# Thresholded attention and tanh-shrink layers: shared tiles of two neighbouring pairs in one duo, and a joint product for both tiles' last keys

## The chip, the cores and the metric

The kernel runs on one core of a Trainium2 chip. The metric is the time of one execution on the device, in microseconds (us), and lower is better. The engines of the core are named as the profile names them: PE is TensorE (PEld its weight loads), DVE is VectorE, ACT is ScalarE, POOL is GpSimd, and SP is the engine whose queue sends nearly all DMAs.

## What is computed

The reference has two parts, one after the other. Attention over 8 batches x 8 heads x 576 positions x 64 dimensions keeps, in each row, only the scores within tau = 0.02 of the row's largest:

```
scores = scale * q @ k.T
thresh = max(scores, -1) - tau
scores = where(scores >= thresh, scores, -1e9)
attn = softmax(scores);  x = attn @ v
```

The result, laid out as 4608 tokens x 512, goes through two layers: `h = x @ w_in` (2048 wide), `g = h - tanh(h)`, `out = g @ w_out`.

## The kernel before

**Pairs and tiles.** Two heads of a batch make a *pair*, so there are 32 pairs. A head has 576 query rows: four tiles of 128 and a remainder of 64. The remainders of the pair's two heads stand together, 64 rows each, in one *shared* tile. So a pair has `TPP` = 9 tiles: in the kernel before j = 0 to 3 (first head), 4 (shared), 5 to 8 (second head). Tile number i counts on over all pairs to 288.

**Steps of a tile.** `scores` (L296) writes a row tile against all 576 keys into PSUM (psS, two buffers, which the transposes of k and q, ps_k and ps_q, use too): q and k are split into two fp16 halves, so a plain tile takes four matmuls (L320), and a shared tile eight with 64 output rows each (L310). VectorE copies the tile out as sc and takes its row maximum (L330). `shift` (L336) makes the threshold nb of it on VectorE (L347). `kink` (L355) runs a very steep Prelu on ScalarE (L367), which leaves z near zero where a score is kept and hugely negative elsewhere. z is then turned so that keys lie on partitions: for the first six pairs (`on_pe`) by PE transposes into psZ (L387), later by a DMA transpose on SP's queue (L375). `weights` (L377) takes the exponential, giving pT (L396 or L404). `attend` (L409) multiplies pT with the values vb, which carry a column of ones so that the row sum comes along (65 columns); the results go to psO, of which there is one buffer. `norm` (L441) divides on VectorE (L447 to L453) into osb, and `emit_x` (L460) turns a pair's osb by PE (psX, L465 and L471) into the layers' input xT and xR (copied by VectorE, L478 and L479).

**Duos.** 576 is four and a half blocks of 128 keys. Two plain tiles therefore lie side by side in one z of 1152 = 9 x 128 columns, called a *duo*: (0,1), (2,3), (5,6), (7,8), kind A the first and B the second. The middle block holds the last 64 keys of both tiles, so vb has two versions of that key block (index 4 and 5), one with zeros in the lower and one in the upper half. A shared tile (kind M) has no partner: its z is padded with hugely negative numbers to 640 columns (tiles zm, L93 to L98), has its own transpose of five blocks and its own exponential of 640 columns. Of a duo, each tile takes five value products of 65 columns, ten in all (L433); the shared tile takes five of 130 columns, for both heads' values at once, of which `own` picks the right head's half (L453).

**The order of the work** is written out by hand: each engine runs its instructions in the order in which the loop over steps s (L681) writes them, for all engines together. Step s holds `shift` of tile s + 7, `scores` of tile s + 8 (`AHEAD`), `kink` of tile s + 5, tanh of the last hidden block (`bend`, L497), `weights` of tile s, one piece of the layers, `shrink` (g on VectorE, L504), the stores that are due, `attend` of tile s - 2 with `norm` and `emit_x`, and then what the plan has for the step (`PREP`, L634): loads of k, q and v, their splitting on POOL, and the transposes `turn` (L242), which for pair p fall on steps 9p - 13 (k) and 9p - 11 (q); q of the odd pairs from 9 on and of pair 30 is turned by DMA instead, at step 9p - 13. (The first 36 tiles run their weights and attend four steps early.)

**The layers.** From pair 4 on, each stretch of 36 steps (four pairs) also works on the batch before: 16 pieces of `hidden` (four matmuls into psH, L488) and 16 of `project` (four into psY, L514), one a step, hidden on even steps, from the stretch's fifth step on; the first four steps have none. psH shares its two buffers with psX. Where a psY is complete, VectorE copies it out (yo, L524). What is left after the last tile, from 466 us, is layers alone.

Of the kernel before, what the change touches and what calls it, by code (L numbers as in the profile page):

```python
# [9 lines left out]
F32 = mybir.dt.float32  # L10
BF16 = mybir.dt.bfloat16
FP16 = mybir.dt.float16
AX = mybir.AxisListType
ALU = mybir.AluOpType
# [4 lines left out]
def kernel(  # L19
# [11 lines left out]
    nc = tc.nc  # L31
    P = 128

    B, H, S, D = q.shape
# [3 lines left out]
    tau = float(tau)  # L38
# [5 lines left out]
    STEEP = 1.0e30  # L44
# [2 lines left out]
    NPAIR = B * HPAIR  # L47
    DM_C = d_model // P
    DF_C = d_ff // P
    TPP = 9  # L50
    NTILE = NPAIR * TPP

# [18 lines left out]
    const = ctx.enter_context(tc.tile_pool(name="const", bufs=1))  # L71
# [11 lines left out]
    NV = 4  # L83
    vbs = []
    for i in range(NV):
        vb = const.tile([P, 2, 6, D + 1], BF16, name=f"vb{i}")
# [2 lines left out]
        nc.gpsimd.memset(vb[0:64, :, 4, D : D + 1], 1.0)  # L89
        nc.gpsimd.memset(vb[64:P, :, 5, D : D + 1], 1.0)  # L90
        vbs.append(vb)

    NM = 2  # L93
    zms = []
    for i in range(NM):
        zm = const.tile([P, 5 * P], BF16, name=f"zm{i}")
        nc.vector.memset(zm[:, S : 5 * P], -STEEP)
        zms.append(zm)  # L98

    mx3 = []
    for i in range(6):
        mx = const.tile([P, 8], F32, name=f"mx{i}")
# [26 lines left out]
    ps_o = pool("ps_o", 1, space=PSUM)  # L131
# [157 lines left out]
    REM = (slice(512, 576), slice(576, 640))  # L289
    scs, mxs, nbs, zs, zts, pts, ops = {}, {}, {}, {}, {}, {}, {}  # L290

    def kind(j):

        return "M" if j == 4 else "A" if j in (0, 2, 5, 7) else "B"

    def scores(i):  # L296
        p, j = divmod(i, TPP)
        qT, kT, kS = mats[p, "q"], mats[p, "k"], mats[p, "ks"]
        ps = ps_big.tile([P, 1024], F32, name="psS", tag="big")
        main, rem, lo = slice(0, 512), slice(512, 576), 0  # L300
        if kind(j) == "B":
            main, rem, lo = slice(512, 1024), slice(448, 512), 448
        if j == 4:
            qrem = REM
            if q_by_dma(p):
                qrem = (slice(512, 640, 2), slice(513, 640, 2))
            for n, kk in enumerate((kT, kS)):
                for dst, srcs in ((main, MAIN), (rem, REM)):
                    for hh in range(2):
                        nc.tensor.matmul(  # L310
                            out=ps[64 * hh : 64 * hh + 64, dst],
                            lhsT=qT[:, qrem[hh]], rhs=kk[:, srcs[hh]],
                            start=(n == 0), stop=(n == 1),
                        )
        else:
            hh = int(j > 4)
            lhs = qT[:, j * P : (j + 1) * P]
            for n, kk in enumerate((kT, kS)):
                for dst, src in ((main, MAIN[hh]), (rem, REM[hh])):
                    nc.tensor.matmul(  # L320
                        out=ps[:, dst], lhsT=lhs, rhs=kk[:, src],
                        start=(n == 0), stop=(n == 1),
                    )
        sc = sc_pool.tile([P, S], F32, name="sc")
        if kind(j) == "B":
            mx = mxs[i] = mxs.pop(i - 1)
        else:
            mx = mxs[i] = mx3[i // 2 % len(mx3)]
        c = int(kind(j) == "B")
        nc.vector.tensor_scalar(  # L330
            out=sc, in0=ps[:, lo : lo + S], scalar1=SC, scalar2=None,
            op0=ALU.mult, op1=ALU.max, accum_out=mx[:, c : c + 1],
        )
        scs[i] = sc

    def shift(i):  # L336

        kd = kind(i % TPP)
        if kd == "A":
            return  # L340
        mx = mxs.pop(i)
        nb = st_pool.tile([P, 9], F32, name="nb", tag="nb")
        o, m = nb[:, 0:1], mx[:, 0:1]
        if kd == "B":
            o = nb.rearrange("p (a b) -> p a b", b=3)[:, :, 0:2]
            m = mx.rearrange("p (a b) -> p a b", b=4)[:, :, 0:3]
        nc.vector.tensor_scalar(  # L347
            out=o, in0=m, scalar1=-1.0, scalar2=tau, op0=ALU.mult, op1=ALU.add
        )
        if kd == "B":  # L350
            nbs[i - 1], nbs[i] = nb[:, 0:1], nb[:, 1:2]
        else:
            nbs[i] = nb[:, 0:1]

    def kink(i):  # L355
        sc, nb = scs.pop(i), nbs.pop(i)
        kd = kind(i % TPP)
        if kd == "B":
            zt = zs.pop(i - 1)
            z = zt[:, S:W]  # L360
        elif kd == "A":
            zt = zs[i] = z_pool.tile([P, W], BF16, name="z")
            z = zt[:, 0:S]
        else:
            zt = zms[i // TPP % NM]
            z = zt[:, 0:S]
        nc.scalar.activation(  # L367
            out=z, in_=sc, func=ACT.Prelu, bias=nb, scale=1.0, alpha=STEEP
        )
        if on_pe(i):  # L370
            zts[i] = zt
        elif kd != "A":
            n = 5 if kd == "M" else TPP
            zts[i] = zt_pool.tile([P, TPP, P], BF16, name="zT")
            nc.sync.dma_start_transpose(out=zts[i][:, 0:n, :], in_=zt)  # L375

    def weights(i):  # L377


        kd = kind(i % TPP)  # L380
        n, off = {"A": (4, 0), "M": (5, 0), "B": (5, 4)}[kd]
        if on_pe(i):
            z = zts.pop(i)
            pl, tag = (ps_h, "h") if i % 2 and i < HPAIR * TPP else (ps_y, "y")
            ps = pl.tile([P, 5 * P], BF16, name="psZ", tag=tag)
            for c in range(n):
                nc.tensor.matmul(  # L387
                    out=ps[:, c * P : (c + 1) * P],
                    lhsT=z[:, (off + c) * P : (off + c + 1) * P],
                    rhs=ident_bf, is_transpose=True, start=True, stop=True,  # L390
                )
            if kd == "B":
                pt = pts.pop(i - 1)
            else:
                pt = p_pool.tile([P, TPP * P], FP16, name="pT")
            nc.scalar.activation(  # L396
                out=pt[:, off * P : (off + n) * P], in_=ps[:, 0 : n * P], func=ACT.Exp
            )
        elif kd == "A":
            return  # L400
        else:
            n += off
            pt = p_pool.tile([P, TPP * P], FP16, name="pT")
            nc.scalar.activation(  # L404
                out=pt[:, 0 : n * P], in_=zts.pop(i)[:, 0:n, :], func=ACT.Exp
            )
        pts[i] = pt

    def attend(i):  # L409

        p, j = divmod(i, TPP)
        kd, vb = kind(j), vbs[p % NV]
        if kd == "A":
            return
        if j in (1, 6):
            ops[p, int(j > 4)] = ps_o.tile([P, 6, D + 1], F32, name="psO", tag="o")
        po = ops[p, int(j > 4)]
        if kd == "M":
            pt = pts.pop(i)

            for c in range(5):
                nc.tensor.matmul(
                    out=po[:, 4:6, :], lhsT=pt[:, c * P : (c + 1) * P],
                    rhs=vb[:, :, c, :], start=(c == 0), stop=(c == 4),
                )
            return
        pt, hh = pts.pop(i), int(j > 4)

        for ab in range(2):
            blocks = [(4 * ab + ab + c, c) for c in range(4)]  # L430
            blocks.append((4, 4 + ab))
            for n, (blk, c) in enumerate(blocks):
                nc.tensor.matmul(  # L433
                    out=po[:, (j - 1 - 5 * hh) + ab, :],
                    lhsT=pt[:, blk * P : (blk + 1) * P], rhs=vb[:, hh, c, :],
                    start=(n == 0), stop=(n == 4),
                )

    osb = {}

    def norm(p, hh):  # L441
        po = ops.pop((p, hh))
        if hh == 0:
            osb[p] = o_pool.tile([P, 5, 2, D], BF16, name="osb")
        n = 5 - hh
        rc = st_pool.tile([P, 5], F32, name="rc", tag="rc")
        nc.vector.reciprocal(out=rc[:, 0:n], in_=po[:, 0:n, D])  # L447
        nc.vector.tensor_tensor(  # L448
            out=osb[p][:, 0:4, hh, :], in0=po[:, 0:4, 0:D],
            in1=rc[:, 0:4].unsqueeze(2).to_broadcast([P, 4, D]), op=ALU.mult,  # L450
        )
        if hh == 0:
            nc.vector.scalar_tensor_tensor(  # L453
                out=osb[p][:, 4, :, :], in0=po[:, 4:6, 0:D], scalar=rc[:, 4:5],
                in1=own, op0=ALU.mult, op1=ALU.mult,
            )
# [224 lines left out]
    for s in range(-AHEAD, NTILE + LAG + 3):  # L681
        p, j = divmod(max(s, 0), TPP)
# [36 lines left out]
        for i in atts.pop(s, []):  # L719
            pp, jj = divmod(i, TPP)  # L720
            if i < NTILE:
                attend(i)
            if i < NTILE and jj in (4, 8):
                norm(pp, int(jj > 4))
            if jj == 1 and pp:
                emit_x(pp - 1)
        for step in plan.pop(s, []):
            step()
# [61 lines left out]
```

## Time and profile before

| | |
|---|---|
| timed runs, us | 537.05, 538.59, 539.47 (median 538.59) |
| profiled execution | 537.19, of which the profile's span is 535.4 |
| granted TensorE clock | 1.0 throughout |
| sc (L330) | 288 of 752 ns, 216.2 us of VectorE |
| z (L367) | 288 of 768 to 770 ns, 218.1 us of ScalarE |
| exp after a DMA transpose (L404) | 104 of 1152 columns, 1153 ns; 26 of 640 columns, 726 ns |
| value products of duos (L433) | 1280 of 65 columns |
| value products of shared tiles (L422) | 160 of 130 columns |
| nb (L347) | 128 for duos, 155 ns; 32 for shared tiles, 144 ns |
| DMA transposes of z (L375) | 104 of duos, 26 of shared tiles |

Each row comes from the groups of instructions by line. The duration of one instruction is longer than what it takes from its engine, because the next one starts before it ends: of ten value products each lasts 193 ns, but they start about 32 ns apart. The profile's list of waits puts idle time down to the work that ended it; the chain that ended last follows the work back from the last instruction.

### The profile page before, as it was taken

The numbers are of one execution on the slowest core, as the hardware profiler recorded it, in microseconds if no ns is written. First come the engines' busy times: TensorE is split into PE (matmuls) and PEld (weight loads), VectorE is DVE, ScalarE is ACT, GpSimd is POOL, SyncE is SP. The second block draws the span as 40 slices with busy tenths as digits, with TensorE's granted clock in tenths as the row PEclk, the third lists the DMA queues.
The fourth block names the chain that finished last, engine by engine and source line by source line (L and its number), as shares of the span: only waits on it lengthen the run. The fifth ranks groups of instructions, "written<-read, shape, count | busy, mean of one in ns | idle before, by whom it ended". The sixth has DMA issues, their size and how long they took to land.

```text
span 535.4 us, 12959 instructions
## 1 busy us (share of the span) xinstructions
PE 506.0 (95%) x4704; PEld 287.7 (54%) x4771; DVE 427.1 (80%) x1201; ACT 437.9 (82%) x630; POOL 290.2 (54%) x390
## 2 busy tenths in 40 slices
PE   5999898999999999999999999999999999999997
PEld 3666565555555555555555555555555455444444
DVE  4999888989888988889888988898888888554440
ACT  4999888999898989899888989898989989543330
POOL 7999996767555666656555755566665620000000
PEclk9999999999999999999999999999999999999999
DMA  7654646999898899889998899998999985401113
GB/s 204 182 185 146 208 155 163 181 183 186 189 191 160 180 197 184 168 182 189 192 184 186 184 193 185 164 180 197 186 168 179 198 148 107 105 21 39 39 41 78
DMA packets 204768, 85.76 MB, mean 160 GB/s; under 512 B 172320, under 2 KB 197152, under 8 KB 204704
## 3 DMA queue, kind: packets, MB, share of 16 engines
q1 hardware_dynamic: 204112, 84.51, 74.8%
q8 instruction: 37, 0.61, 0.5%
q10 hardware_dynamic: 592, 0.43, 0.3%
q14 instruction: 27, 0.22, 0.1%
HBM read 36.70 MB, written 9.44 MB: 86 GB/s over the span
## 4 chain that ended last, share of the span: by engine, by line
PE 71%; DVE 16%; ACT 6%; issue 3%; DMA 3%; POOL 1%; SPq 0%; DVEq 0%; ACTq 0%; POOLq 0%
PE psY L514 20%; PE psH L488 18%; PE psS L320 16%; DVE sc L330 8%; PE psO L433 5%; PE psS L310 3%; DVE g L507 3%; ACT pT L396 3%; PE psHt L488 3%; PE ps_k L234 2%; ACT z L367 2%; DVE kT L257 2%; PE psZ L387 1%; DVE yo L524 1%; PE ps_q L234 1%
## 5 line engine op out<-in xcount | busy, mean ns | idle before, releaser
L330 DVE TENSOR_SCALAR_CACHE_REDUCE sc<-psS 128x576 f32<-128x576 f32 x288 | 216.2, 752 | 23.7 <-PE psS L320 14.2
L367 ACT ACTIVATE z<-sc,nb 128x576 bf16<-128x576 f32 x256 | 193.5, 768 | 19.7 <-DVE nb L347 19.7
L514 PE MATMUL psY<-w_out_sb,g 128*128 128x512 bf16 (+1 forms) x551 | 137.6, 373 | 3.3 <-issue 0.9
L263 POOL COPY kS<-kT 64x1152 f16<-64x1152 f16 x62 | 70.7, 1141 | 128.7 <-DVE nb L347 127.0
L404 ACT ACTIVATE pT<-zT 128x1152 f16<-128x1152 bf16 (+1 forms) x130 | 138.8, 1068 | 0.7 <-DMA zT<-z 0.7
L488 PE MATMUL psH<-xT,w_in_sb 128*128 128x512 bf16 x455 | 119.1, 379 | 3.6 <-DVE g L507 2.3
L320 PE MATMUL psS<-kT,qT 128*128 128x512 f16 (+1 forms) x512 | 104.9, 286 | 7.3 <-DVE sc L330 5.1
L501 ACT ACTIVATE th<-psH 128x512 f32<-128x512 f32 x128 | 75.3, 589 | 36.3 <-PE psH L488 33.9
L320 PEld LDWEIGHTS <-qT 128*128 128x128 f16 x1024 | 72.6, 97 | 57.0 <-issue 10.3
L320 PE MATMUL psS<-kS,qT 128*128 128x512 f16 x496 | 101.4, 286 | 0.2 <-POOL kS L263 0.2
L507 DVE SCALAR_TENSOR_TENSOR g<-th,psH 128x512 bf16<-128x512 f32 x128 | 87.3, 682 | 17.6 <-ACT th L501 17.5
L514 PEld LDWEIGHTS <-g 128*128 128x128 bf16 x592 | 50.7, 98 | 56.9 <-issue 4.0
L488 PEld LDWEIGHTS <-w_in_sb 128*128 128x128 bf16 x576 | 49.2, 98 | 58.2 <-issue 4.5
L433 PEld LDWEIGHTS <-pT 128*128 128x128 f16 x1280 | 55.7, 98 | 25.2 <-issue 1.9
L433 PE MATMUL psO<-vb,pT 128*128 128x65 bf16 x1280 | 61.2, 193 | 0.3
L187 POOL TENSOR_TENSOR qhl<-qraw,qhl 128x576 f16<-128x576 f32 x31 | 39.7, 1280 | 2.6
L187 POOL TENSOR_TENSOR khl<-kraw,khl 128x576 f16<-128x576 f32 x31 | 39.6, 1278 | 2.6
L396 ACT ACTIVATE pT<-psZ 128x640 f16<-128x640 bf16 (+1 forms) x54 | 35.5, 659 | 4.9 <-PE psZ L387 4.5
L257 DVE COPY kT<-ps_k 128x1152 f16<-128x1152 f16 x31 | 23.4, 756 | 13.6 <-PE ps_k L234 13.5
L524 DVE COPY yo<-psY 128x512 f32<-128x512 f32 (+1 forms) x31 | 21.1, 682 | 13.4 <-DMA out_dram<-yo 6.5
L448 DVE TENSOR_TENSOR osb<-psO,rc 128x256 bf16<-128x256 f32 x64 | 27.2, 424 | 2.2
L234 PE MATMUL ps_k<-ident_f,khl 128*128 128x128 f16 x288 | 22.0, 221 | 5.7 <-DVE khl L200 5.7
(78 smaller groups left out, 507.4 us busy)
## 6 DMA issues: line engine op xcount, KB each, us to landing
vraw<-in_v_dram SPq DMA_DIRECT2D x32, 256.0 KB, 3.5
out_dram<-yo SPq DMA_DIRECT2D x32, 256.0 KB, 2.7
kraw<-in_k_dram SPq DMA_DIRECT2D x31, 256.0 KB, 3.2
qraw<-in_q_dram SPq DMA_DIRECT2D x31, 256.0 KB, 3.7
wt<-in_moe_w_in_dram SPq DMA_DIRECT2D x8, 512.0 KB, 4.7
wt<-in_moe_w_out_dram SPq DMA_DIRECT2D x8, 512.0 KB, 4.2
zT<-z SPq DMA_TRANSPOSE x104, 3.5
kraw<-in_k_dram SPq DMA_DIRECT2D x32, 32.0 KB, 2.8
```

Of the source, the lines that this page charges most:

```text
L187: nc.gpsimd.tensor_tensor(out=hl[:, :, 1, :], in0=x, in1=hl[:, :, 0, :], op=ALU.subtract)
L263: nc.gpsimd.tensor_copy(out=o, in_=i)
L320: nc.tensor.matmul(out=ps[:, dst], lhsT=lhs, rhs=kk[:, src], start=(n == 0), stop=(n == 1),)
L330: nc.vector.tensor_scalar(out=sc, in0=ps[:, lo : lo + S], scalar1=SC, scalar2=None, op0=ALU.mult, op1=ALU.max, accum_out=mx[:, c : c + 1],)
L367: nc.scalar.activation(out=z, in_=sc, func=ACT.Prelu, bias=nb, scale=1.0, alpha=STEEP)
L396: nc.scalar.activation(out=pt[:, off * P : (off + n) * P], in_=ps[:, 0 : n * P], func=ACT.Exp)
L404: nc.scalar.activation(out=pt[:, 0 : n * P], in_=zts.pop(i)[:, 0:n, :], func=ACT.Exp)
L433: nc.tensor.matmul(out=po[:, (j - 1 - 5 * hh) + ab, :], lhsT=pt[:, blk * P : (blk + 1) * P], rhs=vb[:, hh, c, :], start=(n == 0), stop=(n ...
L488: nc.tensor.matmul(out=ps, lhsT=w_in_sb[:, c, n * P : (n + 1) * P], rhs=xs[m][:, c, :] if m < B else xR[:, c, :, :], start=(c == 0), stop= ...
L501: nc.scalar.activation(out=th, in_=ps, func=ACT.Tanh)
L507: nc.vector.scalar_tensor_tensor(out=gs[m][:, n, :], in0=th, scalar=-1.0, in1=ps, op0=ALU.mult, op1=ALU.add,)
L514: nc.tensor.matmul(out=ps, lhsT=gs[m][:, n, ms * P : (ms + 1) * P], rhs=w_out_sb[:, n, cols], start=(n == 0), stop=(n == DF_C - 1),)
```

## The change

The kinds now alternate over all tiles: an even i is A and an odd i is B. So that this works out, a pair of even number has its shared tile last (j = 8) and a pair of odd number has it first (j = 0, its plain tiles being j = 1 to 8). The shared tiles of pairs p and p + 1, p even, are thus neighbours, tiles 9p + 8 and 9p + 9, and make a duo like any other. The tiles zm, and what was written for kind M, are gone.

In `attend`, a duo's middle block is multiplied once with both versions of the last key block (130 columns, into both tiles' places in psO) and is the first of nine products instead of two of ten; the other eight only add. A shared duo takes five products of 130 columns for each of its two tiles, as before: those for the even pair as soon as its pT is there, those for the odd pair two steps later, when that pair's first psO is opened, so the shared pT is held for both. The five-wide `norm` (with the shared tile) is now that of the second head in even pairs and of the first head in odd pairs. `emit_x` of an even pair comes at j = 2 of the next pair; that of an odd pair stays at j = 1.

```diff
-    NM = 2
-    zms = []
-    for i in range(NM):
-        zm = const.tile([P, 5 * P], BF16, name=f"zm{i}")
-        nc.vector.memset(zm[:, S : 5 * P], -STEEP)
-        zms.append(zm)
...
-    def kind(j):
-        return "M" if j == 4 else "A" if j in (0, 2, 5, 7) else "B"
+    def kind(i):
+        return "AB"[i % 2]
+
+    def place(i):
+        p, j = divmod(i, TPP)
+        j = j - p % 2
+        return (p, None, 4) if j in (-1, 8) else (p, j // 4, j % 4)
...
-        elif kd != "A":
-            n = 5 if kd == "M" else TPP
+        elif kind(i) == "B":
             zts[i] = zt_pool.tile([P, TPP, P], BF16, name="zT")
-            nc.sync.dma_start_transpose(out=zts[i][:, 0:n, :], in_=zt)
+            nc.sync.dma_start_transpose(out=zts[i], in_=zt)
...
+        p, hh, t = place(i)
+        vb, pt = vbs[p % NV], pts[i]
+        if hh is None:
+            attend_shared(p - 1, 0, pt)
             return
-        pt, hh = pts.pop(i), int(j > 4)
-        for ab in range(2):
-            blocks = [(4 * ab + ab + c, c) for c in range(4)]
-            blocks.append((4, 4 + ab))
-            for n, (blk, c) in enumerate(blocks):
...
+        if t == 1:
+            ops[p, hh] = ps_o.tile([P, 6, D + 1], F32, name="psO", tag="o")
+            if p % 2 and hh == 0:
+                attend_shared(p, 1, pts.pop(i - 2))
+        po = ops[p, hh]
+        nc.tensor.matmul(
+            out=po[:, t - 1 : t + 1, :], lhsT=pt[:, 4 * P : 5 * P],
+            rhs=vb[:, hh, 4:6, :], start=True, stop=False, skip_group_check=True,
+        )
+        for n in range(8):
+            ab, c = divmod(n, 4)
+            blk = 5 * ab + c
+            nc.tensor.matmul(
+                out=po[:, t - 1 + ab, :], lhsT=pt[:, blk * P : (blk + 1) * P],
+                rhs=vb[:, hh, c, :], start=False, stop=(n == 7), skip_group_check=True,
+            )
+        pts.pop(i)
+
+    def attend_shared(p, ab, pt):
+        vb = vbs[p % NV]
+        for n in range(5):
+            blk, c = ((5 * ab + n, n) if n < 4 else (4, 4 + ab))
+            nc.tensor.matmul(
+                out=ops[p, 1 - p % 2][:, 4:6, :], lhsT=pt[:, blk * P : (blk + 1) * P],
+                rhs=vb[:, :, c, :], start=(n == 0), stop=(n == 4),
+            )
...
-            if i < NTILE and jj in (4, 8):
-                norm(pp, int(jj > 4))
-            if jj == 1 and pp:
+                odd = pp % 2
+                if jj == 3 + odd:
+                    norm(pp, 0)
+                elif odd and jj in (0, 8):
+                    norm(pp - (jj == 0), 1)
+            if pp and jj == 1 + pp % 2:
                 emit_x(pp - 1)
```

More of the change, by code (lines that the diff above doesn't have):

```diff
@@ L290 @@
     scs, mxs, nbs, zs, zts, pts, ops = {}, {}, {}, {}, {}, {}, {}
-    def kind(j):
-        return "M" if j == 4 else "A" if j in (0, 2, 5, 7) else "B"
+    def kind(i):
[4 more added lines that the diff above has]
+        return (p, None, 4) if j in (-1, 8) else (p, j // 4, j % 4)
     def scores(i):
-        p, j = divmod(i, TPP)
+        p, hh, t = place(i)
         qT, kT, kS = mats[p, "q"], mats[p, "k"], mats[p, "ks"]
@@ L300, in scores @@
         main, rem, lo = slice(0, 512), slice(512, 576), 0
-        if kind(j) == "B":
+        if kind(i) == "B":
             main, rem, lo = slice(512, 1024), slice(448, 512), 448
-        if j == 4:
+        if hh is None:
             qrem = REM
@@ L315, in scores @@
         else:
-            hh = int(j > 4)
-            lhs = qT[:, j * P : (j + 1) * P]
+            lhs = qT[:, (5 * hh + t) * P : (5 * hh + t + 1) * P]
             for n, kk in enumerate((kT, kS)):
@@ L324, in scores @@
         sc = sc_pool.tile([P, S], F32, name="sc")
-        if kind(j) == "B":
+        if kind(i) == "B":
             mx = mxs[i] = mxs.pop(i - 1)
@@ L328, in scores @@
             mx = mxs[i] = mx3[i // 2 % len(mx3)]
-        c = int(kind(j) == "B")
+        c = int(kind(i) == "B")
         nc.vector.tensor_scalar(
@@ L336, in shift @@
     def shift(i):
-        kd = kind(i % TPP)
-        if kd == "A":
+        if kind(i) == "A":
             return
@@ L342, in shift @@
         nb = st_pool.tile([P, 9], F32, name="nb", tag="nb")
[L343 to L346, printed above, removed]
         nc.vector.tensor_scalar(
-            out=o, in0=m, scalar1=-1.0, scalar2=tau, op0=ALU.mult, op1=ALU.add
-        )
[L350 to L353, printed above, removed]
+            out=nb.rearrange("p (a b) -> p a b", b=3)[:, :, 0:2],
+            in0=mx.rearrange("p (a b) -> p a b", b=4)[:, :, 0:3],
+            scalar1=-1.0, scalar2=tau, op0=ALU.mult, op1=ALU.add,
+        )
+        nbs[i - 1], nbs[i] = nb[:, 0:1], nb[:, 1:2]
     def kink(i):
         sc, nb = scs.pop(i), nbs.pop(i)
-        kd = kind(i % TPP)
-        if kd == "B":
+        if kind(i) == "B":
             zt = zs.pop(i - 1)
             z = zt[:, S:W]
-        elif kd == "A":
+        else:
             zt = zs[i] = z_pool.tile([P, W], BF16, name="z")
-            z = zt[:, 0:S]
-        else:
-            zt = zms[i // TPP % NM]
             z = zt[:, 0:S]
@@ L371, in kink @@
             zts[i] = zt
-        elif kd != "A":
-            n = 5 if kd == "M" else TPP
+        elif kind(i) == "B":
             zts[i] = zt_pool.tile([P, TPP, P], BF16, name="zT")
-            nc.sync.dma_start_transpose(out=zts[i][:, 0:n, :], in_=zt)
+            nc.sync.dma_start_transpose(out=zts[i], in_=zt)
     def weights(i):
-        kd = kind(i % TPP)
-        n, off = {"A": (4, 0), "M": (5, 0), "B": (5, 4)}[kd]
+        kd = kind(i)
+        n, off = {"A": (4, 0), "B": (5, 4)}[kd]
         if on_pe(i):
@@ L409, in attend @@
     def attend(i):
-        p, j = divmod(i, TPP)
-        kd, vb = kind(j), vbs[p % NV]
-        if kd == "A":
+        if kind(i) == "A":
             return
[L415 to L425, printed above, removed]
-            return
-        pt, hh = pts.pop(i), int(j > 4)
-        for ab in range(2):
-            blocks = [(4 * ab + ab + c, c) for c in range(4)]
-            blocks.append((4, 4 + ab))
-            for n, (blk, c) in enumerate(blocks):
[L433 to L437, printed above, removed]
+        p, hh, t = place(i)
+        vb, pt = vbs[p % NV], pts[i]
+        if hh is None:
+            attend_shared(p - 1, 0, pt)
+            return
+        if t == 1:
[23 more added lines that the diff above has]
+            )
     osb = {}
@@ L444, in norm @@
             osb[p] = o_pool.tile([P, 5, 2, D], BF16, name="osb")
-        n = 5 - hh
+        shared = hh != p % 2
+        n = 4 + shared
         rc = st_pool.tile([P, 5], F32, name="rc", tag="rc")
@@ L451, in norm @@
         )
-        if hh == 0:
+        if shared:
             nc.vector.scalar_tensor_tensor(
```

## The prediction

> **What bounds the kernel now.** Read first the engines' shares and the chain that ended last:
>
> ```profile
> PE 506.0 (95%) x4704; PEld 287.7 (54%) x4771; DVE 427.1 (80%) x1201; ACT 437.9 (82%) x630; POOL 290.2 (54%) x390
> ...
> PE 71%; DVE 16%; ACT 6%; issue 3%; DMA 3%; POOL 1%; SPq 0%; DVEq 0%; ACTq 0%; POOLq 0%
> ```
>
> TensorE (PE) leads in both, but an average hides stages, so next the stretches (columns: busy us of PE, weight loads, VectorE, ScalarE, GpSimd; clock; DMA share; GB/s):
>
> ```profile
> 20.00:50.00 30.00, 27.78 (x392) 19.57 (x389) 27.09 (x86) 29.32 (x49) 28.45 (x35) 1.00 0.58 175
> 210.00:270.00 60.00, 58.74 (x558) 33.13 (x566) 52.95 (x152) 54.27 (x76) 35.65 (x45) 1.00 0.92 182
> ```
>
> Up to about 94 us, before the expert layers fill the steps, ScalarE is full (29.3 of 30). From 94 to 466 PE is (58.7 of 60), VectorE has 12% and ScalarE 10% to spare. After 466 only the expert layers are left, which the change doesn't touch. The chain in order of time (start, length, work) gives PE's prices in the middle stage:
>
> ```profile
> 255.27 0.49 PE psS L320 x4
> 255.76 0.86 PE psY L514 x4
> 256.62 0.61 PE psS L310 x8
> 257.23 0.97 PE psH L488 x4
> 258.20 0.32 PE psO L433 x10
> ...
> 260.38 0.29 PE psO L422 x5
> ```
>
> A plain tile's scores cost 0.49, a shared tile's (L310) 0.61, and the four matmuls behind it 0.97 where they take 0.86 elsewhere: a shared tile costs 0.12 + 0.11 = 0.23 us more. A duo's ten value products take 0.32 (0.032 each), a shared tile's five 0.29 (0.058 each).
>
> Every 36 steps (four pairs, 57.97 us: the psH groups at 171.71 and 229.68 in that chain) four steps hold no expert work. There VectorE sets the pace, as PE's timeline shows:
>
> ```profile
> 294.91 0.48 PE L433 MATMUL psO<-vb,pT 128*128 128x65 bf16 x10
> 295.54 0.41 PE L320 MATMUL psS<-kT,qT 128*128 128x512 f16 x2 [0.15 <-DVE sc L330]
> 295.78 0.41 PE L320 MATMUL psS<-kS,qT 128*128 128x512 f16 x2
> 296.41 0.41 PE L320 MATMUL psS<-kT,qT 128*128 128x512 f16 x2 [0.22 <-DVE sc L330]
> ```
>
> By starts, 294.91 + 0.32 = 295.23 against 295.54 is 0.31 us lost, 295.54 + 0.49 = 296.03 against 296.41 another 0.38: some 0.7 us of free PE time in each such gap. Two more stalls matter below:
>
> ```profile
> 212.82 1.02 PE L488 MATMUL psH<-xT,w_in_sb 128*128 128x512 bf16 x4 [0.32 <-DVE g L507]
> ```
>
> ```profile
> 424.58 0.42 PE L320 MATMUL psS<-kT,qT 128*128 128x512 f16 x2 [0.89 <-DMA qT<-qhl]
> ```
>
> ```profile
> 417.80 1.94 SPq L375 DMA_TRANSPOSE zT<-z  x1
> 419.84 0.53 SPq L527 DMA_DIRECT2D out_dram<-yo  x1
> 420.48 1.62 SPq L246 DMA_TRANSPOSE qT<-qhl  x1
> ```
>
> The first comes at step 22 of the 36, just after psX (step 21), where psH needs a buffer that the g of that same step frees. The second is pair 30's q, transposed by DMA; SP works in order and sent it late, behind a zT. PE's preceding psY group ended at 423.53, so it lost 1.05 us.
>
> **What the Trainium skill says.** "TensorE: Matmul & The Clock Gate", Back-to-back issue gap: warm, a matmul of N columns takes about N/2.4 + 2.5 ns, so 30 for 65 columns and 57 for 130; the trace has 32 and 58. Two 65-column products joined into one save almost nothing. "TensorEngine Tiling (Array Packing)", Restrictions: column tiling disables fast weight load; the trace agrees (64-column weight loads of L310 110 ns, 128-column ones 97) and shows the price as the 0.23 above. "PSUM — Partial Sum Buffer", The four PSUM rules: a starting matmul clears written-marks in the whole bank, not data. So the joint product must come first, with later ones only accumulating; it costs no time, and no run here shows it. "Perfetto Trace Analysis", Identifying the Most-Contended Engine, warns that matmul busy time overstates; hence I price by starts.
>
> **The change part by part** (on the profiled span of 535.4; the timed runs' median is 538.59, 0.6% above, and I scale by that).
>
> 1. *Value products.* Per duo 10 x 0.032 = 0.32 becomes 0.058 + 8 x 0.032 = 0.314: -0.006 x 128 duos = **-0.8 us**. Bounds: 0 if the joint one gains nothing; -4.1 if its second 65 columns were free (128 x 0.032). I take the measured spacing; the shared tile's chain of five shows no penalty for adding to what was just written.
>
> 2. *ScalarE, VectorE, DMA savings.* In 26 pairs two 640-wide exps (2 x 726 ns) become one of 1152 (1153): 13 x 0.30 = 3.9 us of ScalarE. Nb: 32 of 144 ns become 16 of 155: 2.1 us of VectorE. SP issues 117 nine-block transposes for 104 plus 26 of five. All lies beside PE, at the shares above: nothing, except in the ScalarE-full start. There 3 times two 640-wide exps (706) become 512 + 640 (599 + 706): 3 x 0.107 = **-0.3**, and three PE transposes (0.06 each) go too, hidden.
>
> 3. *Where shared tiles stand.* Scores run 8 tiles ahead. Before, pair p's shared tile is scored at step 9p - 4: steps 5, 14, 23 and 32 of every 36, all among expert work. After, those of pairs p and p+1 (p even) come at 9p and 9p + 1: steps 0, 1 and 18, 19. Steps 0 and 1 have no expert work, and there two of them need 2 x 0.23 = 0.46 of the 0.7 PE loses anyway. In the stage with expert work (steps 36 to 287) the PE-bound steps held 27 shared tiles and now hold 14: -13 x 0.23 = **-3.0 us**. Bounds: 0 if VectorE's pace is what counts around the gap too; -3.0 if all is hidden. K and kS of both heads were needed by these steps already; GpSimd's queue keeps its order.
>
> 4. *Pair 30's q.* The zT in front of it moves one step earlier, ahead of the q loads; after, loads and a store stand between, which wait less. Bounds 0 and -1.05; I take **-0.7**.
>
> 5. *psX of even pairs.* Emitted one step later: steps 13 and 31 instead of 12 and 30. At 12 and 30 the next psH took psX's own buffer; now, as at step 21, it waits for that step's g, and all expert work queues behind it. From the end of psY to that psH the stall above implies 1.36 us (269.43 to 270.79 in the next period); PE now has 0.29 + 0.31 + 0.25 + 0.49 = 1.34 to do at step 13, more at 31. Bounds 0 and 14 x 0.32 = +4.5 us; I take 0.04 a time, **+0.6**.
>
> 6. *Other waits.* The shared duo's pT is read by two steps 2 apart; its buffer returns every 6 steps and is free after 4, so exp keeps two steps (3 us). psO still has two steps between norm and next use. Two memsets at the start, about 0.2 us of VectorE, lie beside the first loads. All 0.
>
> Sum: -0.8 - 0.3 - 3.0 - 0.7 + 0.6 = -4.2, so 531.2, or 534.4 against the median.
>
> **The rivals.** *Shared tiles' place is worth nothing*: PE saves in steps 5 to 32 only what it then waits for VectorE. For it: the chain runs on VectorE from 289.5 to 296.4. Against: PE does not stall until 295.5. Sum -1.2: 537.4.
>
> *VectorE's crowding in odd pairs makes it slower.* The five-wide norm of the even pair now falls into the odd pair's step 2, psX copies into 4, kT into 5, the odd pair's own five-wide norm into 6. By starts: two norms 1.64, copies 0.46, kT 0.67, five sc 3.35, g 1.5, nb 0.18, yo 0.61: 8.4 us, against PE's 5 x (0.49 + 0.86) + 0.58 + 0.62 + 0.25 + 0.50 = 8.7 in the same five steps. The worst five before (even pair, steps 3 to 7) are 8.3 against 9.1. If dependences keep VectorE idle there for 0.8, PE waits 0.5 in each of 14 odd pairs: +7.0, so 541.4. It decides from 4.2/14 = 0.30 per odd pair. Against it: two score buffers, and kT sat idle 1.1 us for PE before.
>
> **How the numbers follow.** My sum 0.60 (532 to 536 of its own, as items 1, 4 and 5 vary), no worth in the place 0.27 (536 to 539), crowding 0.13 (540 to 543). The range 531.5 to 539.5 leaves out crowding and the far edge. About 0.5% (535.9 and 541.3) is what a measurement of this kernel can tell: faster 0.56, same 0.32, slower 0.12.
>
> **What would show it.** Right: nine value products in 0.31; the 36-step period at about 57.4; no stall of the third score in the gap; no qT wait near 423. Wrong: psH waiting for g after all psX; scores in odd pairs waiting for sc; a period of 58 or more.

## The result and the profile after

The changed kernel is slower: a median of 540.31 us (six runs, 539.57 to 540.91) against 537.97 (six runs of the kernel before, the three of the table above among them), a ratio of 1.0042 with a 95% interval of 1.0025 to 1.0059. The forecast was 534.4, faster, with a range of 531.5 to 539.5. The page of the profiled execution, whose span is 538.8 (535.4 before), shows less work and a longer span:

```profile
PE 508.4 (94%) x4640; PEld 289.0 (54%) x4640; DVE 424.5 (79%) x1183; ACT 435.2 (81%) x617; POOL 290.2 (54%) x390
...
PE 64%; DVE 12%; ACT 8%; POOL 5%; DMA 5%; issue 4%; SPq 1%; DVEq 0%; ACTq 0%; POOLq 0%
```

Read this against the same two lines of before. PE has fewer recorded instructions, VectorE 2.6 us and ScalarE 2.7 us less work, as the change should bring. But PE's share of the chain fell from 71 to 64%: PE waits more. For whom, these shares don't tell. ScalarE (6 to 8), GpSimd (1 to 5) and DMA (3 to 5) grew and VectorE fell (16 to 12), yet GpSimd's part lies before 94 us, outside the middle stage, and the largest new wait there will turn out to be one for VectorE. The stretches show even less:

```profile
20.00:50.00 30.00, 27.04 (x376) 19.32 (x373) 25.93 (x80) 29.16 (x49) 28.45 (x35) 1.00 0.61 181
210.00:270.00 60.00, 58.72 (x536) 32.93 (x535) 52.09 (x149) 53.29 (x74) 35.79 (x46) 1.00 0.88 179
```

PE is as busy from 210 to 270 as before (58.72 of 60 against 58.74): a matmul that starts late still follows others closely, and its length covers most of a short wait. The start times say more. One mark comes once per pair, the first psX matmul, and from it the time of 36 steps can be taken:

| 36 steps, from psX to psX | pair 12 | 13 | 14 | 15 | sum |
|---|---|---|---|---|---|
| before | 15.44 | 14.72 | 15.70 | 12.11 | 57.97 |
| changed | 17.29 | 13.47 | 17.10 | 10.62 | 58.48 |

(psX of even pairs moved by a step, so only the sums compare.) Where nothing else disturbs them, all periods of the middle stage are like this: 0.51 us lost in 36 steps, and I had forecast 57.4. In the profiled executions the psX of pair 7 comes 1.1 us earlier than before (122.2 against 123.3), that of pair 27 comes 3.0 later (416.4 against 413.4), and at the last pair it is 3.1. So the middle loses 4.1, and the end is as it was. The microsecond gained at the start is no more than two profiles of the same opening differ by: the psX of pair 5 comes at 96.1 here and at 97.2 in f1_q_early (below), whose program is the same up to there. Of the 4.1, the regular loss makes 5 x 0.51 = 2.6; single longer stretches make most of the rest (for pairs 8, 20 and 25: 18.05, 17.73 and 13.99 where their like take 17.29 and 13.48).

The chain inside one such period (start, length, work) names the largest new wait:

```profile
184.66 0.69 DVE yo L522
185.35 0.68 DVE g L505
186.04 0.10 DVE rc L445
186.14 0.02 issue
186.17 0.04 DVE osb L446
186.20 0.31 issue
186.51 0.76 DVE kT L251
187.27 0.04 issue
187.31 0.65 PE psS L319 x4
```

This is step 5 of the 36, in an even pair. VectorE runs in the order in which its instructions are written: yo, g, then the pair's first norm (rc and osb, L445 and L446), and only then kT, the copy that empties PSUM of the k transposes. PE's scores of step 7 need that buffer. Before, this norm (five-wide then) came a step later, and kT followed g at once, as VectorE's timeline of the kernel before shows:

```profile
186.14 0.75 DVE L257 COPY kT<-ps_k 128x1152 f16<-128x1152 f16 x1
...
187.54 0.19 DVE L447 RECIPROCAL rc<-psO 128x5 f32<-128x5 f32 x1
```

PE's own timeline of the changed kernel has the price of this and of the other waits:

```profile
185.77 1.03 PE L486 MATMUL psH<-xT,w_in_sb 128*128 128x512 bf16 x4
187.31 0.41 PE L319 MATMUL psS<-kT,qT 128*128 128x512 f16 x2 [0.51 <-DVE kT L251]
...
199.29 0.41 PE L319 MATMUL psS<-kS,qT 128*128 128x512 f16 x2
199.73 1.02 PE L486 MATMUL psH<-xT,w_in_sb 128*128 128x512 bf16 x4
...
239.67 0.23 PE L413 MATMUL psO<-vb,pT 128*128 128x130 bf16 x1 [0.38 <-ACT pT L392]
```

By starts: psH takes 0.86, so PE was ready at 186.63 and began at 187.31, **0.68 us** lost. Scores take 0.245 a pair of records, so psH behind psX could have begun at 199.54 and began at 199.73: 0.19, and 0.16 at 230.28; the listing puts no wait beside either. The last line is the gap without expert work: there PE now loses 0.54 waiting for ScalarE's pT, and at the two places where it lost 0.31 and 0.38 to VectorE's sc before, 0.12 and 0.20 are left. In pairs 8 and 20 the extra time of the longer stretches falls on the wait for kT again (1.36 and 1.12 us in place of 0.68; the chain leads from kT back over g, tanh and z to a zT that came late); in pair 25 PE waits for qT.

What was forecast as a gain is there too. Chain of the same kernel, the two shared tiles of pairs 14 and 15, which fall among expert work:

```profile
205.94 0.61 PE psS L310 x8
206.55 0.97 PE psH L486 x4
207.52 0.62 PE psS L310 x8
208.14 0.97 PE psY L512 x4
```

A shared tile costs there what it did before, 0.12 + 0.11 us more than a plain one, and there are two in 36 steps instead of four.

### The profile page after: what moved, and what is told of

The parts are those of the page before. It is cut to its first block, busy times and chain, and to the rows that moved or that the text cites. A ratio compares the mean times of both kernels' runs of the same rounds, so it can differ in the third digit from the quotient of the medians.

```text
span 538.8 us, 12796 instructions
## 1 busy us (share of the span) xinstructions
PE 508.4 (94%) x4640; PEld 289.0 (54%) x4640; DVE 424.5 (79%) x1183; ACT 435.2 (81%) x617; POOL 290.2 (54%) x390
## 4 chain that ended last, share of the span: by engine, by line
PE 64%; DVE 12%; ACT 8%; POOL 5%; DMA 5%; issue 4%; SPq 1%; DVEq 0%; ACTq 0%; POOLq 0%
PE psY L512 19%; PE psH L486 17%; PE psS L319 14%; ACT z L356 3%; PE psO L420 3%; DVE g L505 3%; DVE sc L329 3%; PE psHt L486 3%; DVE kT L251 2%; ACT pT L392 2%; PE psS L310 2%; PE ps_k L228 2%; DMA qT<-qhl 2%; DVE yo L522 2%; DMA zT<-z 2%
## 5 line engine op out<-in xcount | busy, mean ns | idle before, releaser
L356 ACT ACTIVATE z<-sc,nb 128x576 bf16<-128x576 f32 x288 | 216.9, 770 | 39.0 <-DVE nb L341 38.5
L512 PE MATMUL psY<-w_out_sb,g 128*128 128x512 bf16 (+1 forms) x592 | 145.9, 373 | 0.8 <-DVE yo L522 0.8
L392 ACT ACTIVATE pT<-zT 128x1152 f16<-128x1152 bf16 x117 | 134.9, 1153 | 2.1 <-DMA zT<-z 2.1
L486 PE MATMUL psH<-xT,w_in_sb 128*128 128x512 bf16 x480 | 123.3, 379 | 2.5 <-DVE g L505 2.3
L319 PEld LDWEIGHTS <-qT 128*128 128x128 f16 x1024 | 74.2, 98 | 65.3 <-issue 13.6
L420 PE MATMUL psO<-vb,pT 128*128 128x65 bf16 x1024 | 53.3, 194 | 0.0
L420 PEld LDWEIGHTS <-pT 128*128 128x128 f16 x1024 | 44.2, 98 | 9.7
L384 ACT ACTIVATE pT<-psZ 128x512 f16<-128x512 bf16 (+1 forms) x54 | 35.0, 652 | 4.6 <-PE psZ L375 4.0
L413 PE MATMUL psO<-vb,pT 128*128 128x130 bf16 x128 | 28.2, 221 | 1.7 <-ACT pT L392 1.5
L446 DVE TENSOR_TENSOR osb<-psO,rc 128x256 bf16<-128x256 f32 x64 | 27.2, 424 | 2.2
```

The costliest lines, as they stand in the source:

```text
L319: nc.tensor.matmul(out=ps[:, dst], lhsT=lhs, rhs=kk[:, src], start=(n == 0), stop=(n == 1),)
L356: nc.scalar.activation(out=z, in_=sc, func=ACT.Prelu, bias=nb, scale=1.0, alpha=STEEP)
L384: nc.scalar.activation(out=pt[:, off * P : (off + n) * P], in_=ps[:, 0 : n * P], func=ACT.Exp)
L392: nc.scalar.activation(out=pt[:, 0 : n * P], in_=zts.pop(i)[:, 0:n, :], func=ACT.Exp)
L420: nc.tensor.matmul(out=po[:, t - 1 + ab, :], lhsT=pt[:, blk * P : (blk + 1) * P], rhs=vb[:, hh, c, :], start=False, stop=(n == 7), skip_gr ...
L486: nc.tensor.matmul(out=ps, lhsT=w_in_sb[:, c, n * P : (n + 1) * P], rhs=xs[m][:, c, :] if m < B else xR[:, c, :, :], start=(c == 0), stop= ...
```

## Experiments

All kernels ran beside the kernel before; medians of that ranged from 537.6 to 538.1, so ratios compare best.

**1. The norm behind the k transposes (e1_norm_late).** From the changed kernel:

```diff
                 if jj == 3 + odd:
-                    norm(pp, 0)
+                    if odd:
+                        norm(pp, 0)
+                    else:
+                        late.append(pp)
...
         for step in plan.pop(s, []):
             step()
+        while late:
+            norm(late.pop(), 0)
```

> The changed kernel, with the first norm of even pairs issued after the k transposes of the same step instead of ahead of them. Theory N (that norm stands ahead of kT on VectorE, PE's next scores wait for kT, 0.68 us once every 36 steps): the wait falls to about 0.1, so 7 x 0.55 = 3.9 us less than the changed kernel's 540.3, near 536.4. Rival Y (kT is late because of yo and g, not the norm): under 1 us less, 539.5 or more. Rival P (the time comes back where ScalarE paces the four steps without expert work): 540, with a longer gap there.

Measured: 537.89, ratio 1.0003 (0.9992 to 1.0014), 2.4 us less than the changed kernel (2.1 by the ratios). VectorE's timeline:

```profile
184.43 0.69 DVE L505 SCALAR_TENSOR_TENSOR g<-th,psH 128x512 bf16<-128x512 f32 x1
185.04 0.75 DVE L251 COPY kT<-ps_k 128x1152 f16<-128x1152 f16 x1
185.71 0.17 DVE L445 RECIPROCAL rc<-psO 128x4 f32<-128x4 f32 x1
185.91 0.42 DVE L446 TENSOR_TENSOR osb<-psO,rc 128x256 bf16<-128x256 f32 x1
```

kT now follows g at once. PE's scores of step 7 began at 185.84, ready at 184.85 + 0.86 = 185.71: 0.13 is left of 0.68, and 36 steps take 57.94. Theory N holds for the wait, to the hundredth (16.74 us from pair 11's psX to pair 12's, instead of 17.29); Y falls. But only 2.4 of 3.9 us arrive at the end. In this profile, pair 28's stretch, in which PE waits for pair 30's qT, took 17.80 (17.34 in the changed kernel): by starts PE lost 1.54 us to qT in place of 0.54, which gives back 1.0. The psX of pair 4 came 0.5 later, within the spread of the start.

**2. psX behind the psH of an even step (e2_emit_even).**

```diff
-            if pp and jj == 1 + pp % 2:
+            if pp and jj == 1 + 2 * (pp % 2):
                 emit_x(pp - 1)
```

> The changed kernel, with psX of even pairs one step later still (j = 3 of the next pair), so that it stands at an even step, behind that step's psH. Theory X (at steps 13 and 31 psH waits for the g of its own step because psX sits between them; measured 0.19 and 0.17 us, once each per 36 steps): 7 x 0.36 = 2.5 us less, near 537.8. Rival: the waits are VectorE's general lateness in odd pairs and move to another instruction: 540.

Measured: 538.74, ratio 1.0023 (1.0014 to 1.0032), 1.6 us less (1.0 by the ratios, whose intervals overlap); 36 steps take 58.14, 0.34 less, as Theory X said. Of the 2.5 us that it promised in all, less arrives. PE's timeline at step 14:

```profile
199.21 1.03 PE L486 MATMUL psH<-xT,w_in_sb 128*128 128x512 bf16 x4
200.07 0.39 PE L463 MATMUL psX<-ident_bf,osb 128*128 128x128 bf16 x4
200.30 0.19 PE L469 MATMUL psX<-fold,osb 128*128 128x64 bf16 x1
200.33 0.67 PE L228 MATMUL ps_k<-ident_f,khl 128*128 128x128 f16 x9
```

No start is late by more than 0.01 here.

**3. nb right behind sc (e3_nb_early).**

```diff
-        if 0 <= s + AHEAD - 1 < NTILE:
-            shift(s + AHEAD - 1)
         if 0 <= s + AHEAD < NTILE:
             scores(s + AHEAD)
+            shift(s + AHEAD)
```

> The changed kernel, with nb made right after the duo's second sc instead of at the start of the next step. Theory A (ScalarE's z of the duo's first tile waits for nb, which stands behind g, norms and copies; so ScalarE enters the four steps without expert work with no lead, and PE waits there for pT, 0.5 us per 36 steps): waits of z for nb fall from 38 to under 20 us and the time by 7 x 0.3 = 2 us, near 538. Rival: ScalarE has slack, its waits cost nothing[...]: unchanged or up to 1 us slower.

Measured: 540.39, ratio 1.0051 (1.0039 to 1.0063): the total stays. Yet the cause is real. ScalarE's timeline of the changed kernel as the gap begins:

```profile
234.92 0.78 ACT L356 ACTIVATE z<-sc,nb 128x576 bf16<-128x576 f32 x1 [0.84 <-DVE nb L341]
235.60 0.58 ACT L499 ACTIVATE th<-psH 128x512 f32<-128x512 f32 x1
236.08 1.15 ACT L392 ACTIVATE pT<-zT 128x1152 f16<-128x1152 bf16 x1
```

In the list of waits of the changed kernel z waits for nb twice as long as before:

```profile
ACT z L356 <- DVE nb L341: 38.5, 58, 1.2
```

(us in total, times, longest; 19.7 us in 25 times before). Every duo's first z needs the nb of its second tile, which is made a step ahead of it and stood behind the five-wide norm here. Before, one tile in nine was a shared one with an nb of its own and a step more to spare, and it stood at this place in every fourth pair. With the early nb no such wait is left in the list of the middle stage, and the gap (from psO behind its last psY to psX) took 3.77 us: 3.98 in the changed kernel, 3.75 before. But the following pair's steps took 0.1 more, and in this profile the psX of pair 4 came 1.2 later, so nothing reached the end. ScalarE's idle time did not go either, it moved: between 130 and 415 us tanh now waits for psH 50 times, 28.9 us in all, a wait that the changed kernel's list does not have there. Theory A is right about the gap and wrong about the total.

**4. The joint product alone (e4_joint_alone).** In the kernel before, each duo gets the nine products of the changed kernel; all else stays.

> The kernel before, with the joint product of both tiles' last keys alone (nine value products per duo instead of ten), shared tiles as they were. By my sum 128 x 0.006 = 0.8 us less than before, so a ratio of 0.9985; if the second half of the joint product were free, 4.1 us less (0.992); if it costs PE something not seen, above 1.0.

Measured: 536.89, ratio 0.9985 (0.9977 to 0.9992), what the sum said, 0.8 us less (0.4 to 1.2 by the interval). Its 36 steps take 57.92, 0.05 less than before, where 16 duos of 0.006 would make 0.10. So this half of the change is a small gain, and the rest costs about 3 us.

**5. The new order without the merged duo (e5_order_alone).** The changed kernel, in which the shared tiles of pairs p and p + 1 stay neighbours but each keeps its own z, transpose and exponential:

```diff
     def kind(i):
-        return "AB"[i % 2]
+        return "M" if place(i)[1] is None else "AB"[i % 2]
...
+        elif kind(i) == "M":
+            zt = zms[i % 2]
+            z = zt[:, 0:S]
...
-        elif kind(i) == "B":
+        elif kind(i) != "A":
+            n = 5 if kind(i) == "M" else TPP
```

> The changed kernel's order of tiles, its joint product, norms and psX, but its two neighbouring shared tiles are not merged: each has its own padded z of 640 columns, transpose and exponential again. Theory: the loss comes from the order (norm ahead of kT, psX at odd steps), so this takes what the changed kernel takes, 540.3 within 1 us, with the same 0.68 us wait for kT every 36 steps. Rival: merging itself costs (the pT held for two pairs, nb of two shared tiles at once, the joint transpose): then this is 2 us or more faster than the changed kernel, about 538.

Measured: 545.24, ratio 1.0146 (1.0124 to 1.0168). Neither expectation: it is 5 us slower than the changed kernel. The rival is out: in this order merging does not cost, it saves. The chain has the same norm ahead of kT, and 36 steps take 58.72. Much of the rest is in single stretches of the profile, whose run (548.28) was the longest of six: pair 28's took 20.96 us, with DMA of qT the largest item of the chain there (20.4% of 421 to 442 us). With 26 transposes for 13, SP's queue may be what makes q later; that was not tried by itself.

**6. The mends together.** c_norm_emit holds 1 and 2, c_all also 3; c_norm_emit_q holds 1 and 2 and, as the run after it, the edit

```diff
-        d = 5 if q_by_dma(p) else 3 - (p == 1)
+        d = 6 if q_by_dma(p) else 3 - (p == 1)
```

> The changed kernel with both mends, the norm behind the k transposes and psX one step later. If the two costs add, 36 steps take 58.48 - 0.55 - 0.34 = 57.59, 7 x 0.89 = 6.2 us less than the changed kernel: 534.1. If what the norm's mend gave back elsewhere (2.4 us came of 3.9) is given back again: 536.3.

> Both mends and the early nb. My prediction had 57.4 us for 36 steps; if the place of the shared tiles is worth what it said once the new waits are gone, the gap without expert work costs PE no more than before (psO behind the last psY to psX: 3.75 us before, 3.98 in the changed kernel) and 36 steps take 57.4, 533 in all. If the gap is paced by ScalarE or VectorE so that two shared tiles there cost their 0.23 each, 57.6 or more and 534.5 or more.

> Both mends, and the DMA transposes of q (12 odd pairs and pair 30) issued one step earlier. If waits for qT take back part of the gain (pair 30's stretch took 17.8 us where others took 16.7 in the kernel with the norm mended), 1 us less than the kernel with both mends. If SP then stands waiting for qhl with zT behind it, or DMA is full anyway: no less.

> The changed kernel with the DMA transposes of q issued one step earlier and nothing else. The regular stretches account for 5 x 0.51 = 2.6 of the 4.1 us lost between the psX of pairs 7 and 27, single longer stretches (waits for qT and zT) for the rest. If those for qT are a cost of the change, about 1 us less than the changed kernel: 539.3. If they only shift: 540.3.

| | median us | ratio (95%) | 36 steps |
|---|---|---|---|
| c_norm_emit | 536.64 | 0.9976 (0.9967 to 0.9986) | 57.58 |
| c_all | 536.38 | 0.9978 (0.9967 to 0.9990) | 57.49 |
| c_norm_emit_q | 535.74 | 0.9968 (0.9956 to 0.9980) | 57.58 |
| f1_q_early (changed kernel, q early) | 539.64 | 1.0030 (1.0018 to 1.0043) | 58.48 |

The two costs add: 57.58 where 57.59 was expected. With the nb early as well it is 57.49, near the forecast of 57.4, and z's waits for nb are all but gone; the list of waits of c_all, middle stage:

```profile
ACT z L356 <- DVE nb L341: 1.9, 11, 0.2
```

As totals, both mends together bring 3.7 us of the 6.2 expected, so the second expectation ("given back again") is nearer, and c_all stayed 3.4 above its 533. The early q is worth about 0.7 to 0.9 us in medians, in both kernels, and the intervals of each couple overlap: pair 28's stretch went from 17.34 to 16.79 and from 18.34 to 17.59 us, which is what it takes without a wait (its like, less 0.50 for a q that PE does not transpose there). In the same two profiles pair 8's stretch grew, from 18.05 to 19.05 and from 18.08 to 19.91.

**7. Versions that beat both.** In every kernel so far psH also waits at step 22 for the g behind step 21's psX (0.48 us by starts). Moving that psX a step on as well:

```diff
-            if pp and jj == 1 + pp % 2:
+            if pp and jj == (1, 3, 2, 3)[pp % 4]:
```

f2_best has this, the late norm and the early q; f3_best_nb the early nb besides. f4_before_mended gives the kernel before what helps it too: the joint product, the early q, and `jj == (2 if pp % 4 == 2 else 1)`.

> Norm behind the k transposes, q early, psX of even pairs at j = 3, and psX of the odd pair before a pair p with p mod 4 = 2 at j = 2 instead of 1 (step 22 instead of 21), which takes away the 0.48 us that psH waits for g there in every kernel so far: 7 x 0.48 = 3.4 us less than the 535.7 without that: 532.4. If VectorE has no room, the wait moves on: 535.

> The same with the early nb, which left the total as it was twice: 532.4 again, or up to 0.7 us less as the gap without expert work shortens by 0.2 each time and the steps after it lengthen by 0.1.

> The kernel before, with its own shared tiles and order, with what helps it too: the joint product (0.8), psX at step 22 instead of 21 (3.4) and q one step earlier (0 to 0.4). 537.6 - 4.3 = 533.3. Against the kernel with the shared duo and all mends (532.4 expected) the difference is what the shared duo is worth by itself: 0.46 us per 36 steps less 0.15 still waited for kT, 2 us, if my price for a shared tile's place holds; nothing if it doesn't.

| | median us | ratio (95%) | 36 steps |
|---|---|---|---|
| f2_best | 531.90 | 0.9881 (0.9865 to 0.9896) | 57.11 |
| f3_best_nb | 529.71 | 0.9846 (0.9833 to 0.9858) | 57.04 |
| f4_before_mended | 532.57 | 0.9897 (0.9883 to 0.9911) | 57.43 |

f3_best_nb is 1.5% faster than the kernel before. Against f4_before_mended, f2_best takes 0.32 us less for 36 steps, most of the 0.46 at which the place of its shared tiles was priced. In medians the two are 0.7 us apart and their intervals overlap. f3_best_nb is 2.9 us ahead, but the kernel before was not tried with the early nb, so what the shared duo by itself is worth in the total is not shown. Why the early nb pays 2 us here and nothing in the changed kernel stays open too. The profiles can't tell: the one of f2_best is of the fastest of its five runs (530.32) and the one of f3_best_nb of the slowest of its four (530.87), with 57.04 us in two of its four periods and 57.4 in the others.

## Why the prediction was wrong, step by step

1. *Value products, -0.8.* Right in the total, 0.9985 alone, and in the chain, 0.06 + 0.25 = 0.31 us a duo; the 36 steps show half of it.
2. *Savings beside PE.* Right that they hide: 2.6 us less VectorE and 2.7 us less ScalarE work did not shorten the middle stage. The -0.3 at the start can't be told from the spread of the start between profiles (1.1 us).
3. *Place of the shared tiles, -3.0.* The mechanism holds, 2 x 0.23 = 0.46 in 36 steps, and the 36 steps of c_all and f2_best agree with it. (Of the 0.23, the 0.11 lies by starts in the group ahead of the shared tile and not in the one behind: in PE's timeline of before, psY starts at 255.59 and the shared tile at 256.55, 0.96 later. The sum is the same.) In the changed kernel itself half of it was lost: the gap took 0.23 more, because ScalarE entered it late. The free 0.7 us that the prediction counted there were free for PE only as long as ScalarE kept its lead, and it drew that lead from a shared tile's early nb that the change took away. No item priced that.
4. *Pair 30's q, -0.7.* The mechanism was right and the size a little too large: by starts PE lost 0.54 us to this qT (ready at 426.89, began at 427.43) in place of 1.05, so 0.5 saved. But single waits for zT and qT grew elsewhere (1.7 us in the three stretches named above), which no item had. They differ from kernel to kernel; their cause is not settled beyond the 0.7 to 0.9 that an earlier q returns.
5. *psX of even pairs, +0.6.* The mechanism was right and the size too small: 0.04 taken, 0.19 and 0.16 measured, 7 x 0.35 = 2.5 us instead of 0.6. The bound (0.32) held it. What was mis-sized is the time from the end of psY to that psH: 1.36 was taken over from step 22, and it is 1.54 (198.19 to 199.73) and 1.51 (228.77 to 230.28) here, against the same 1.34 of work both times; that PE had more to do at step 31 was wrong.
6. *Other waits, "All 0".* **This step failed.** The list had psO, pT and the memsets, but not the norm of even pairs, which moves from j = 4 to j = 3 and thereby into step 5, ahead of kT in VectorE's queue and behind yo and g. It costs 0.68 us in every 36 steps, 7 x 0.68 = 4.8 us, more than the whole forecast gain; moving that one call behind the transposes returns 0.55 of it in every 36 steps and 2.1 to 2.4 us of the total.

The rival "crowding" had the right engine, the right kind of wait and the right instruments, but looked in the wrong pairs. It added up five steps of the odd pairs, which got the second wide norm, and there kT came in time; the even pairs lost work in that sum (the wide norm went), and what hurt them was the position of a smaller one. The account for 36 steps, by starts: +0.68 (kT), +0.35 (psX), +0.23 (gap, its two shared tiles included), -0.46 (place), -0.10 (products, of which e4_joint_alone showed 0.05), and -0.22 for two waits of before that are gone (0.10 ahead of the shared tile at step 5, 0.12 behind ps_q at step 7). That is +0.48, against 0.51 measured.

## What to carry to other kernels

When a change moves a call from one step to another, write out, for every engine that it issues to, the instructions of the new step in order, and ask of each one behind it who waits for that; sums of work over a few steps cannot show that one short instruction now stands ahead of the one that frees a buffer. Idle time that one engine has in a stage can be spent only as far as the next engine's lead reaches, so price that lead too. And if a change is right in its main idea but slower, look for the calls that came along with it: here moving four calls (norm, psX, nb and the transposes of q), without touching the idea, turned 0.4% slower into 1.5% faster. Then ask what the old kernel gains from the like moves: here 1.0% (f4_before_mended), so most of the 1.5% is not owed to the idea.

## What the runs showed that was not expected

Two shared tiles in a row cost less than two apart. In the gap of the changed kernel nothing stands between them, as PE's timeline shows:

```profile
236.01 0.22 PE L413 MATMUL psO<-vb,pT 128*128 128x130 bf16 x1
...
236.41 0.44 PE L310 MATMUL psS<-kT,qT 128*64 128x512 f16 x4
...
236.93 0.42 PE L310 MATMUL psS<-kT,qT 128*64 128x512 f16 x4
...
237.52 0.23 PE L413 MATMUL psO<-vb,pT 128*128 128x130 bf16 x1
```

The second begins 0.52 us after the first, against 0.49 for a plain tile; among expert work each costs 0.23 more. By starts, the rest of the price lies ahead of the first, where psO takes 0.40 in place of 0.31, and in the second, which takes 0.59. So most of it seems to be paid where the shape changes, into the 64-row matmuls and out of them, and not in the group. That goes against the prediction's reading, which saw in the 0.23 the price of slower weight loads: the first of the two tiles has the same eight loads and pays 0.03. No run tested this by itself.
